# Storing the soft max's split parts from GpSimd's DMA queue, with a new set of stream priorities

## The chip, the cores and the metric

The kernel runs on one core of one Trainium2 chip. The metric is the device time of one execution in microseconds (us), lower is better. The engines are called as in the profile: PE is TensorE's matmul and PEld its weight load, DVE is VectorE, ACT is ScalarE, POOL is GpSimd, SP is SyncE. SPq and POOLq are the instruction queues of SP and POOL where they issue DMAs.

## What is computed

Three layers follow one another. An attention with landmarks (Nystrom) over 4 batches and 8 heads of 576 tokens of 64, a mixture of 8 experts of which each token goes to the best one, and a dense layer with a leaky activation:

```
q_lm, k_lm = means of 18 tokens, 32 landmarks          # per batch and head
A  = softmax(q    @ k_lm.T / 8)                        # 576 x 32
Bm = softmax(q_lm @ k_lm.T / 8)                        # 32 x 32
C  = softmax(q_lm @ k.T    / 8)                        # 32 x 576
Z  = Bm.T / (norm1 * norminf);  6 times: Z = 2 Z - Z @ Bm @ Z
x  = A @ Z @ C @ v                                     # 2304 tokens of 512
e  = argmax(x @ w_gate);  keep the first `capacity` tokens of each expert
y  = gate * (relu(x @ w1[e]) @ w2[e])                  # 512 -> 1024 -> 512
h  = y @ w_in;  g = max(h, 0) + alpha * min(h, 0)      # 512 -> 2048
out = g @ w_out                                        # 2048 -> 512
```

w_in and w_out arrive as 64-bit floats, and the kernel narrows them itself.

## The kernel before

Work is written as streams: Python generators that yield one operation at a time (an instruction with its engine and an estimate of its duration). `Plan.run` lays the streams out ahead of time into one fixed order for each engine. Of the operations that could start at about the same planned time on an engine it takes that of the stream with the lowest rank (ranks closer than 30 ns of planned start compete; otherwise the earlier start wins). Each engine and each DMA queue then runs its order strictly front to back, and an instruction that waits holds everything behind it. So a changed rank, a changed engine or a changed duration moves instructions on all engines. Line L74, at which nearly all rows stand, is the helper that issues every operation.

The stages of the first pass are:

- **Attention.** For each batch b four head pairs are turned (`turn`: loads of q and k come in from SP, PE transposes them, ACT moves them to `qkT`, PE averages the landmarks, DVE copies those to `half`, which PE transposes too). For each of the 8 groups (b, g) of four heads, `attend_c` makes C, Bm and C @ v (rows named mx, nm, EC, EB, CT, Ys), and `attend_a` makes A. The latter's steps are, in order: scores into PSUM (`big`); DVE transposes them to `T1` (rows say T); DVE takes the maxima `amx`; an engine subtracts them (T<-T,amx); ACT takes the exponential; DVE sums (`asum`) and scales (T<-T,asum); DVE transposes to `AT`; ACT rounds AT to 16 bits (`parts[:, 0]`); an engine subtracts to get the rest (`parts[:, 1]`); a DMA stores both parts to `xdram` in DRAM. Batch 0 keeps its parts in `xT` itself, so its rows say xT for parts. xdram is read back only when a later expert is fetched (`prefetch`, xT<-xdram).
- **post0** (`attention_post([0])`) runs Z's six steps for batch 0 (rows RW), makes the router's logits (mm<-Gm,AT), finds the expert of the first token (`e0`), and routes. From `e0` on SP may load that expert's W1 (stream `weights`), and `landmark_rows` multiplies W1 with the landmarks' values (big<-W,MT); for that it needs both `big` buffers of PSUM, which the attention's groups use too. `post` does the same for the three other batches.
- **moe_h, moe_y, moe2_h, moe2_out** (stream `first`, then `out`) are the expert and the dense layer for batch 0. `moe_h` multiplies xT with W1's rows (MW); `moe_y` multiplies with W2 and turns its five tiles to `yT`; `moe2_h` takes 16 slices f of w_in against yT, in two column ranges: A (256 columns, tiles 0 and 1) and B (320 columns, the other tiles). `columns(..., ahead)` gives the order: the first `ahead` slices in range A, the same slices in range B, then both ranges slice by slice. `moe2_out` multiplies with w_out (WO).
- **w_in and w_out** are prepared beside all that: 64-bit words come in by SP (the first ten rows to a stage in hgA by stream `early`, the others to `st`), DVE narrows them (int32 rows), ACT takes sums of squares, and `split` makes two 16-bit halves of each pair. A split of kind "d" is one ACT instruction and one DVE instruction; kind "a" is two ACT instructions and one on POOL. `convert(..., low)` gives pair k the kind `low[k % len(low)]`.
- **The loop** then repeats expert and dense layer for each further pair of batch and expert that has tokens (twice with these inputs), with an order of its own. While the first pass's `moe2_out` runs, `first_next`, `next_w1` and `next_w2` fetch and split the weights of the loop's first round.

In `run`, the streams' ranks are given as numbers; the attention's are RANKS[b][g] - 1.768 for `attend_c`, RANKS[b][g] + 4.328 for `attend_a`, and RANKS[b][hp // 2] + 0.943 for `turn`.

Of the kernel before, what the change touches and what calls it, by code (L numbers as in the profile page):

```python
# [10 lines left out]
I32 = mybir.dt.int32  # L11
AF = mybir.ActivationFunctionType
ALU = mybir.AluOpType
# [4 lines left out]
P = 128  # L18
TP = 64
TJ = 9  # L20
BLOCKS = (8, 1, 3, 5, 7, 0, 2, 4, 6)
LM = 32
AT0 = 512 - 10 * LM - LM
RANKS = [[2.735, 1.638], [2.359, 2.122], [2.325, 2.315], [3.168, 3.56]]
MAXF = 3.0e38
GAP = 2
EARLY = 12
# [338 lines left out]
class Kernel:  # L366
# [124 lines left out]
    def loads(self):  # L491

        for b in range(self.B):
            for hp in range(self.H // 2):
                for nm, src in (("k", self.k), ("q", self.q), ("v", self.v)):
                    self.raw[nm, b, hp] = t = yield Get(self.S["v" if nm == "v" else "qk"])
                    yield self.dq.dma_start(t, src[b, 2 * hp : 2 * hp + 2].rearrange("h (p j) d -> (h p) j d", j=TJ))
                    self.have.add((nm, b, hp))
                    if (nm, b, hp) == ('v', 0, 0):
                        self.tc.prologue_barrier()  # L500
# [156 lines left out]
    def attend_a(self, b, g):  # L657

        act, dve = self.act, self.dve

        def t(name, n):
            return self.ap.tile([P, n], F32, tag=name, name=f"{name}{b}{g}", bufs=2)

        yield self.until(("T", b, 2 * g), ("T", b, 2 * g + 1))
        T1 = yield Get(self.S["T1"])
        SA = yield Get(self.big)
        SAf = SA.rearrange("p a n -> p (a n)")
        yield self.scores(SAf, b, g, 1, 0, False)
        yield from self.scored(b, g)
        yield dve.transpose(T1, SAf[:, AT0 + LM : 768])  # L670
        yield Put(SA)
        T13 = T1.rearrange("p (c m) -> p c m", m=32)
        amx, asum = t("amx", 18), t("asum", 18)
        yield dve.tensor_reduce(amx, T13, axis=AX.X, op=ALU.max)
        yield (self.gp, dve)[1].tensor_tensor(T13, T13, amx.unsqueeze(2).to_broadcast([P, 18, 32]), op=ALU.subtract)
        yield act.activation(T1, T1, AF.Exp, scale=0.125)
        yield dve.tensor_reduce(asum, T13, axis=AX.X, op=ALU.add)
        yield dve.tensor_scalar(asum, asum, 1e-9, 1.0 / ASCALE, op0=ALU.add, op1=ALU.mult)
        yield dve.reciprocal(asum, asum)
        yield (self.gp, dve)[1].tensor_tensor(T13, T13, asum.unsqueeze(2).to_broadcast([P, 18, 32]), op=ALU.mult)  # L680
        self.AT[b, g] = AT = yield Get(self.S["AT"])
        yield dve.transpose(AT, T1)
        yield Put(T1)
        self.have.add(("A", b, g))

        parts = self.xT[:, g] if b == 0 else (yield Get(self.S["parts"]))
        yield act.copy(parts[:, 0], AT)
        yield (self.gp, dve)[0].tensor_tensor(parts[:, 1], AT, parts[:, 0], op=ALU.subtract)
        self.have.add(("P", b, g))
        yield self.dq.dma_start(self.xdram[b][:, g], parts).after(1.0)  # L690
        if b:
            yield Put(parts)
        self.have.add(("stored", b, g))

    def attention_post(self, bs):

        pe, act, dve, E = self.pe, self.act, self.dve, self.E
        a2 = self.a2
        b = bs[0]
# [58 lines left out]
        for it in range(6):  # L758
            ps = yield Get(self.mm)
            rp = ps[:, : 64 * G].rearrange("p (g m) -> p g m", g=G)  # L760
            n = 1 if it == 5 else 2
# [15 lines left out]
        for _ in range(2):  # L777
            x = yield Get(self.mm)
# [22 lines left out]
        for _ in range(2):  # L801
            x = yield Get(self.mm)
# [26 lines left out]
        for n, bb in enumerate(bs):  # L829
            yield self.until(("A", bb, 0), ("A", bb, 1))  # L830
            AT = [self.AT[bb, g] for g in range(2)]
# [11 lines left out]
        self.have.add(("x", bs[-1]))  # L843
        if b:
            yield self.until(("routed", 0))
            self.streams["post"].own = 3.503
        yield from self.route(bs, L)

    @staticmethod
# [335 lines left out]
    def early(self):  # L1185


        src, n = self.source_in, self.n_early
        stage = self.hg[0].rearrange("p k a n -> p (k a n)").bitcast(I32)
        stage = [stage[:, 2048 * k : 2048 * k + 2048].rearrange("p (k n two) -> p k n two", k=2, two=2) for k in range(2)]  # L1190
        loaded, used = set(), set()

        def loads():
            for i in range(0, n, 2):
                yield Until(lambda: i < 4 or i - 4 in used)
                for k in range(2):
                    yield self.dq.dma_start(stage[i // 2 % 2][:, k].rearrange("p n two -> p (n two)"), src(i + k).bitcast(I32)).after(6.0)
                loaded.add(i)

        yield Fork(loads())  # L1200
        kids = []
        for i in range(0, n, 2):
            yield Until(lambda: i in loaded)
            yield from self.narrow(stage[i // 2 % 2], self.pair("wi", i))
            used.add(i)
            kids.append((yield Fork(self.squares("wi", i))))
        yield ended(kids)
        self.have.add("early")
# [213 lines left out]
    def moe2_h(self, first=False):  # L1422
        act, dve, hg = self.act, self.dve, self.hg
# [18 lines left out]
            yield Put(ps)  # L1442

        self.h = {}
        for x in self.columns("wi", 16, self.tiles, 5 if first else 4):
            if isinstance(x, Until):
                yield x
                continue
            if x[1]:
                self.have.add("wide")  # L1450
            ps = yield Get(self.mm)
            yield self.product(ps, *x)
            self.h[x[:2]] = yield Fork(activated(ps, *x))
# [91 lines left out]

    def weight_in(self):
        yield self.until("rooms", "early")
        yield from self.weight2("wi", self.source_in, self.amax, 'dad', self.n_early)

    def source_in(self, i):  # L1550

# [58 lines left out]
    def run(self):  # L1610
# [14 lines left out]
        with tc.manual_schedule(engines={ET.PE, ET.DVE, ET.Activation, ET.Pool, ET.SP}):  # L1625
# [19 lines left out]
                parts=Slots(self.a2, "parts", [P, 2, 576], F16, bufs=2),  # L1645
                AT=Slots(self.a2, "AT", [P, 576], bufs=6),
# [4 lines left out]
            for _ in range(10):  # L1651
# [1 line left out]
            self.streams = {  # L1653
                "loads": Stream(self.loads(), 0),
                "turn": Stream(self.turn(), 2),
                "constants": Stream(self.constants(), 8.156),
                "post0": Stream(self.attention_post([0]), 2.155),
                "first": Stream(self.pre(), 3.29),
                "weights": Stream(self.weights(), 8.016),
                "rooms": Stream(self.rooms(), 9.297),  # L1660
                "post": Stream(self.attention_post(list(range(1, self.B))), 3.108),
                "early": Stream(self.early(), 11.284),
                "wi": Stream(self.weight_in(), 8.393),
                "wo": Stream(self.weight_out(), 10.574),
                "clear": Stream(self.clear(), 2.147),
                "experts": Stream(self.experts(), 2.517),
                "out": Stream(self.first_out(), 4.43),
                "next": Stream(self.first_next(), 3.207),
                "next_w1": Stream(self.next_w1_late(), 2.351),
                "next_w2": Stream(self.next_w2('d'), 3.573),  # L1670
            }
            for b in range(self.B):
                for g in range(2):
# [8 lines left out]
        n = nc.values_load(self.lst[0:1, 0:1], min_val=0, max_val=self.PAIRS - 1)  # L1682
# [34 lines left out]
```

## Time and profile before

| | us |
|---|---|
| median of 3 runs | 559.45 |
| lowest, highest run | 558.52, 567.44 |
| profiled execution, its own time | 559.79 |
| span of the profiled execution | 558.1 |
| PE busy in the span | 524.8 |
| DVE busy | 307.5 |
| ACT busy | 266.9 |
| POOL busy | 54.7 |

The span is what the trace covers; the 1.7 us between it and the execution's own time lie around the program. Busy times are sums of instruction durations; PE's instructions are pipelined, so that a busy PE need not be at its peak. In rows of instructions "x6" is a count, "<-" stands between what is written and what is read, and a bracket tells how long the engine sat idle before the instruction and what ended that. PEclk is the granted clock of TensorE as a share of full speed.

### The profile page before, as it was taken

The numbers are of one execution on the slowest core, as the hardware profiler recorded it, in microseconds if no ns is written. First come the engines' busy times: TensorE is split into PE (matmuls) and PEld (weight loads), VectorE is DVE, ScalarE is ACT, GpSimd is POOL, SyncE is SP. The second block draws the span as 40 slices with busy tenths as digits, with TensorE's granted clock in tenths as the row PEclk, the third lists the DMA queues.
The fourth block names the chain that finished last, engine by engine and source line by source line (L and its number), as shares of the span: only waits on it lengthen the run. The fifth ranks groups of instructions, "written<-read, shape, count | busy, mean of one in ns | idle before, by whom it ended". The sixth has DMA issues, their size and how long they took to land.

```text
span 558.1 us, 13933 instructions
## 1 busy us (share of the span) xinstructions
PE 524.8 (94%) x5750; PEld 350.4 (63%) x5750; DVE 307.5 (55%) x744; ACT 266.9 (48%) x581; POOL 54.7 (10%) x78
## 2 busy tenths in 40 slices
PE   8798898898999998999999999999999999999995
PEld 6576676476449786544675667754466566775444
DVE  1877778878899998906052459630004355962000
ACT  4564545685476656756043397520013349751000
POOL 4100000100013432101000000001010000000101
PEclk9988879999999999999999999999999999999999
DMA  8858666714649630656000320000005050000000
GB/s 281 247 172 292 205 211 188 236 55 152 228 153 315 191 137 2 172 196 175 38 11 1 119 76 1 1 0 20 38 31 156 1 176 19 1 1 1 38 20 30
DMA packets 36396, 61.21 MB, mean 110 GB/s; under 512 B 6032, under 2 KB 15632, under 8 KB 36336
## 3 DMA queue, kind: packets, MB, share of 16 engines
q1 hardware_dynamic: 35232, 56.80, 32.2%
q0 software_dynamic: 1104, 3.54, 1.7%
q8 instruction: 46, 0.75, 0.6%
q14 instruction: 14, 0.11, 0.1%
HBM read 49.50 MB, written 10.62 MB: 108 GB/s over the span
## 4 chain that ended last, share of the span: by engine, by line
PE 66%; DVE 15%; issue 7%; DMA 6%; ACT 3%; SPq 2%; POOL 0%; POOLq 0%; ACTq 0%; DVEq 0%
PE mm L74 63%; PE big L74 2%; DMA st<-in_moe_w_in 2%; DVE W L74 2%; DMA out<-st,idxc 2%; DMA qk<-in_k 2%; SPq L74 2%; DVE MW L74 1%; DVE WIa L74 1%; DVE WIb L74 1%; DVE mm L74 1%; PE mm L1619 1%; DVE hgA L74 1%; ACT junk L74 1%; DVE g L74 1%
## 5 line engine op out<-in xcount | busy, mean ns | idle before, releaser
L74 PEld LDWEIGHTS <-hgA 128*128 128x128 f16 (+1 forms) x864 | 71.0, 102 | 66.6 <-issue 3.8
L74 PE MATMUL mm<-yT,WIa 128*128 128x256 f16 (+1 forms) x864 | 109.2, 286 | 3.5 <-DVE MW L74 1.3
L74 PEld LDWEIGHTS <-WIa 128*128 128x128 f16 x864 | 83.5, 98 | 27.3 <-issue 4.7
L74 PE MATMUL mm<-WO,hgA 128*128 128x512 f16 (+1 forms) x432 | 73.0, 344 | 0.4 <-issue 0.4
L74 PE MATMUL mm<-W,hgA 128*128 128x512 f16 (+1 forms) x432 | 73.3, 344 | 0.0
L74 PE MATMUL mm<-WO,hgB 128*128 128x512 f16 (+1 forms) x432 | 72.6, 344 | 0.0
L74 ACT ACTIVATE st<-mm,fac 128x512 f32<-128x512 f32 (+1 forms) x15 | 9.7, 644 | 106.2 <-PE mm L74 106.2
L74 PEld LDWEIGHTS <-hgB 128*128 128x128 f16 (+1 forms) x432 | 36.1, 102 | 33.7
L74 ACT ACTIVATE g<-mm 128x256 f32<-128x256 f32 (+1 forms) x96 | 39.3, 414 | 12.5 <-PE mm L74 11.4
L74 DVE SCALAR_TENSOR_TENSOR mm<-g,oma,mm 128x256 f32<-128x256 f32 (+1 forms) x80 | 40.3, 514 | 3.8 <-ACT g L74 2.5
L74 PE MATMUL mm<-xT,MW 128*128 128x320 f16 (+1 forms) x288 | 37.1, 286 | 4.8 <-DVE hgA L74 2.5
L74 POOL DMA_INDIRECT out<-st,idxc x12 | 12.2, 1015 | 297.1 <-ACT st L74 277.5
L74 PE MATMUL mm<-yT,WIb 128*128 128x256 f16 (+1 forms) x288 | 36.2, 286 | 0.4 <-DVE hgB L74 0.4
L74 PEld LDWEIGHTS <-MW 128*128 128x128 f16 x288 | 27.7, 98 | 12.7 <-issue 3.3
L74 DVE COPY idxc<-idxn 128x5 int32<-128x5 int32 x2 | 0.3, 172 | 64.0 <-issue 46.3
L74 PE MATMUL mm<-id,qk 128*128 128x128 f32 x160 | 28.0, 311 | 7.3 <-DVE half L74 3.4
L74 ACT COPY qkT<-mm 128x512 f32<-128x512 f32 (+1 forms) x48 | 25.4, 551 | 18.3 <-PE mm L74 18.0
L74 ACT ACTIVATE junk<-mm 128x512 bf16<-128x512 f32 (+1 forms) x27 | 15.5, 572 | 39.1 <-PE mm L74 38.8
L74 PEld LDWEIGHTS <-WIb 128*128 128x128 f16 x288 | 28.1, 98 | 7.5 <-issue 0.4
L74 PEld LDWEIGHTS mm<-id,qk 128*128 128x128 f32 x160 | 20.4, 157 | 11.5 <-DVE half L74 6.6
L74 ACT ACTIVATE hgA<-mm 128x256 f16<-128x256 f32 (+1 forms) x48 | 19.5, 411 | 17.0 <-PE mm L74 16.9
L74 DVE SCALAR_TENSOR_TENSOR hgA<-mm,hgA 128x256 f16<-128x256 f32 (+1 forms) x48 | 21.4, 455 | 10.1 <-ACT hgA L74 10.0
(284 smaller groups left out, 715.0 us busy)
## 6 DMA issues: line engine op xcount, KB each, us to landing
W<-in_moe_w SPq DMA_DIRECT2D x8, 1024.0 KB, 6.9
st<-in_moe_w_out SPq DMA_DIRECT2D x16, 512.0 KB, 4.1
hgA<-in_moe_w_in SPq DMA_DIRECT2D x10, 512.0 KB, 6.5
qk<-in_k SPq DMA_DIRECT2D x16, 288.0 KB, 4.5
qk<-in_q SPq DMA_DIRECT2D x16, 288.0 KB, 4.9
v<-in_v SPq DMA_DIRECT2D x16, 288.0 KB, 4.4
out<-zero SPq DMA_DIRECT2D x18, 256.0 KB, 4.5
W<-in_moe_w SPq DMA_DIRECT2D x8, 512.0 KB, 4.5
```

The costliest lines, as they stand in the source:

```text
L74: r = getattr(self.lane.engine, name)(*a, **k)
L1619: nc.tensor.matmul(o[:, :256], self.ones16, self.zero.bitcast(F16), start=True, stop=True)
```

## The change

Of the instructions, six places change. Expressions of the form `(self.dq, self.gp)[i]` pick SP's queue for 0 and POOL's for 1; `nm == ""` is never true.

1. `attend_a`: the store of the parts goes from SP's queue to POOL's (8 DMAs).
2. `attend_a`: the subtraction of the maxima goes from DVE to POOL (8 instructions), and that which makes the lower part goes from POOL to DVE (8 instructions).
3. `moe2_h` of the first pass: `ahead` is 3 in place of 5.
4. `weight_in`: w_in's eight pairs are split "d" throughout, in place of "d", "a", "d" in turn (the pairs 1, 4 and 7 change).
5. `next_w2`: W2's four pairs are split "d", "a" in turn, in place of "d" throughout (the pairs 1 and 3 change).
6. Ranks: the attention's groups (0, 0), (1, 0) and (1, 1), and eleven of the streams.

The lines in `loads` and `early` change in form only.

```diff
-RANKS = [[2.735, 1.638], [2.359, 2.122], [2.325, 2.315], [3.168, 3.56]]
+RANKS = [[2.837, 1.638], [3.158, 2.149], [2.325, 2.315], [3.168, 3.56]]
...
-                    yield self.dq.dma_start(t, src[b, 2 * hp : 2 * hp + 2].rearrange("h (p j) d -> (h p) j d", j=TJ))
+                    yield (self.dq, self.gp)[nm == ""].dma_start(t, src[b, 2 * hp : 2 * hp + 2].rearrange("h (p j) d -> (h p) j d", j=TJ))
...
-        yield (self.gp, dve)[1].tensor_tensor(T13, T13, amx.unsqueeze(2).to_broadcast([P, 18, 32]), op=ALU.subtract)
+        yield (self.gp, dve)[0].tensor_tensor(T13, T13, amx.unsqueeze(2).to_broadcast([P, 18, 32]), op=ALU.subtract)
...
-        yield (self.gp, dve)[0].tensor_tensor(parts[:, 1], AT, parts[:, 0], op=ALU.subtract)
+        yield (self.gp, dve)[1].tensor_tensor(parts[:, 1], AT, parts[:, 0], op=ALU.subtract)
         self.have.add(("P", b, g))
-        yield self.dq.dma_start(self.xdram[b][:, g], parts).after(1.0)
+        yield (self.dq, self.gp)[1].dma_start(self.xdram[b][:, g], parts).after(1.0)
...
-            self.streams["post"].own = 3.503
+            self.streams["post"].own = 3.568
...
-        for x in self.columns("wi", 16, self.tiles, 5 if first else 4):
+        for x in self.columns("wi", 16, self.tiles, 3 if first else 4):
...
-        yield from self.weight2("wi", self.source_in, self.amax, 'dad', self.n_early)
+        yield from self.weight2("wi", self.source_in, self.amax, 'd', self.n_early)
...
-                "constants": Stream(self.constants(), 8.156),
-                "post0": Stream(self.attention_post([0]), 2.155),
+                "constants": Stream(self.constants(), 8.105),
+                "post0": Stream(self.attention_post([0]), 3.27),
...
-                "post": Stream(self.attention_post(list(range(1, self.B))), 3.108),
-                "early": Stream(self.early(), 11.284),
+                "post": Stream(self.attention_post(list(range(1, self.B))), 3.015),
+                "early": Stream(self.early(), 11.316),
...
-                "wo": Stream(self.weight_out(), 10.574),
-                "clear": Stream(self.clear(), 2.147),
-                "experts": Stream(self.experts(), 2.517),
-                "out": Stream(self.first_out(), 4.43),
-                "next": Stream(self.first_next(), 3.207),
+                "wo": Stream(self.weight_out(), 10.863),
+                "clear": Stream(self.clear(), 2.619),
+                "experts": Stream(self.experts(), 2.117),
+                "out": Stream(self.first_out(), 7.555),
+                "next": Stream(self.first_next(), 2.2),
...
-                "next_w2": Stream(self.next_w2('d'), 3.573),
+                "next_w2": Stream(self.next_w2('da'), 2.369),
```

## Rows read from the trace of the kernel before

**Rows 1.** Busy time of each engine by stage, in the order of the columns: the stretch (us from the span's start), its length, busy time and count of PE, PEld, DVE, ACT and POOL, the granted clock, the DMA engines' share, GB/s.

```profile
20.00:90.00 70.00, 60.37 (x1285) 46.55 (x1286) 52.48 (x145) 35.38 (x84) 7.10 (x6) 0.85 0.69 222
...
141.00:168.00 27.00, 25.75 (x215) 13.52 (x214) 24.46 (x46) 16.26 (x31) 2.17 (x1) 1.00 0.56 199
168.00:228.60 60.60, 58.12 (x557) 46.72 (x553) 56.17 (x135) 40.28 (x89) 20.15 (x18) 1.00 0.51 157
228.60:278.60 50.00, 49.31 (x326) 24.73 (x323) 17.85 (x28) 23.20 (x37) 5.02 (x5) 1.00 0.49 150
278.60:558.10 279.50, 270.65 (x1986) 172.83 (x1986) 107.13 (x274) 107.35 (x250) 10.65 (x11) 1.00 0.11 37
```

**Rows 2.** The chain of work that ended last, its longest pieces from moe2_h's end on: start, length, what.

```profile
217.75 60.18 PE mm L74 x413
...
278.62 25.64 PE mm L74 x201
...
369.18 45.71 PE mm L74 x282
```

**Rows 3.** What SP's queue waited for over the whole run: in total, times, longest; then SP's timeline around batch 2's first store.

```profile
SPq L74 <- PE mm L74: 69.8, 19, 9.8
SPq L74 <- POOL parts L74: 28.6, 6, 10.2
```

```profile
79.96 0.38 SPq L74 DMA_DIRECT2D qk<-in_q  x1
84.17 0.34 SPq L74 DMA_DIRECT2D xdram<-parts  x1
85.62 1.31 SPq L74 DMA_DIRECT2D W<-in_moe_w  x2
```

**Rows 4.** POOL's groups of instructions, kept apart by shape: count, busy us in total, mean ns of one, idle time before them.

```profile
L74 POOL DMA_INDIRECT out<-st,idxc x12 | 12.2, 1015 | 297.1 <-ACT st L74 277.5 <-DMA W<-in_moe_w 11.0 <-DMA out<-st,idxc 8.6
L74 POOL TENSOR_TENSOR parts<-AT,parts 128x576 f16<-128x576 f32 x6 | 7.7, 1279 | 72.7 <-ACT parts L74 72.7
L74 POOL TENSOR_TENSOR WIa<-WIa 128x1024 f16<-128x1024 f32 x2 | 4.9, 2454 | 45.2 <-ACT WIa L74 45.2
L74 POOL TENSOR_TENSOR WIb<-WIb 128x1024 f16<-128x1024 f32 x1 | 2.2, 2224 | 0.8 <-PE mm L74 0.8
```

**Rows 5.** The instructions that touch T, amx and xdram, by tile: count, shortest/median/longest in ns, first and last start.

```profile
L74 DVE TENSOR_TENSOR T<-T,amx x8: 735/758/760, 16.7 to 109.0; 128x576 f32<-128x576 f32 x8
L74 SPq DMA_DIRECT2D xdram<-parts x6: 343/344/350, 52.9 to 118.6; - x6
L74 SPq DMA_DIRECT2D xT<-xdram x1: 345/345/345, 237.5 to 237.5; - x1
```

**Rows 6.** DVE's timeline in the attention: the transposes that free T1 in the groups (2, 0) and (2, 1) (AT<-T), and those that fill it again in the last two groups (T<-big).

```profile
78.90 0.76 DVE L74 STREAM_TRANSPOSE AT<-T 128x576 f32<-128x576 f32 x1
95.62 0.78 DVE L74 STREAM_TRANSPOSE AT<-T 128x576 f32<-128x576 f32 x1
98.64 0.77 DVE L74 STREAM_TRANSPOSE T<-big 128x576 f32<-128x576 f32 x1
107.29 0.77 DVE L74 STREAM_TRANSPOSE T<-big 128x576 f32<-128x576 f32 x1
```

**Rows 7.** Where a DVE instruction that is short elsewhere takes long beside one of POOL: nm and fac by tile (ns, shortest/median/longest), the same for W<-st,W, and the timelines of POOL and DVE.

```profile
L74 DVE TENSOR_SCALAR nm<-mx x8: 169/441/893, 13.5 to 106.9; 128x2 f32<-128x2 f32 x8
L74 DVE SCALAR_TENSOR_TENSOR fac<-gate,pyr,wfac x5: 200/207/1481, 152.5 to 178.7; 128x1 f32<-128x1 f32 x5
L74 DVE SCALAR_TENSOR_TENSOR W<-st,W x10: 1207/1224/2490, 150.7 to 192.1; 128x1024 int32<-128x1024 int32 x10
```

```profile
163.09 2.17 POOL L74 TENSOR_TENSOR WIa<-WIa 128x1024 f16<-128x1024 f32 x1 [44.55 <-ACT WIa L74]
174.09 2.73 POOL L74 TENSOR_TENSOR WIa<-WIa 128x1024 f16<-128x1024 f32 x1 [0.69 <-ACT WIa L74]
163.86 2.49 DVE L74 SCALAR_TENSOR_TENSOR W<-st,W 128x1024 int32<-128x1024 int32 x1
175.36 1.48 DVE L74 SCALAR_TENSOR_TENSOR fac<-gate,pyr,wfac 128x1 f32<-128x1 f32 x1
```

**Rows 8.** The two kinds of split, DVE's and ACT's share, by shape: count, busy us, mean ns.

```profile
L74 DVE SCALAR_TENSOR_TENSOR WIa<-WIa,s_wi 128x1024 f16<-128x1024 f32 x3 | 3.8, 1274 | 0.0
L74 ACT CAST WIa<-WIa 128x1024 f16<-128x1024 f32 x2 | 2.1, 1040 | 0.8 <-DVE WIa L74 0.8
```

**Rows 9.** The start of moe2_h on PE and DVE: range A's second and third products, the logits, the last tile of yT, and the block of products behind them.

```profile
176.39 1.49 PE L74 MATMUL mm<-yT,WIa 128*128 128x256 f16 x12
178.03 2.26 PE L74 MATMUL mm<-Gm,AT 128*64 128x8 f32 x36
180.23 12.25 PE L74 MATMUL mm<-yT,WIa 128*128 128x256 f16 x96
178.28 0.47 DVE L74 COPY yT<-mm 128x256 f16<-128x256 f16 x2
```

**Rows 10.** What PE and its weight loads waited for in the attention (0 to 108 us), in total, times, longest; then the granted clock of two stretches of 10 us (columns as in rows 1).

```profile
PE mm L74 <- DVE half L74: 3.4, 5, 1.6
PEld mm L74 <- DVE half L74: 6.6, 9, 1.7
```

```profile
70.00:80.00 10.00, 8.84 (x198) 7.34 (x193) 9.23 (x31) 3.85 (x8) 0.00 (x0) 0.79 0.74 225
80.00:90.00 10.00, 10.00 (x154) 7.65 (x154) 5.28 (x24) 4.45 (x11) 1.28 (x1) 0.70 0.54 171
```

**Rows 11.** post0's end and what hangs on it: e0 on DVE, W1's last two loads on SP, the product that needs them on PE.

```profile
76.55 0.14 DVE L74 TENSOR_SCALAR e0i<-m 1x1 int32<-1x1 f32 x1
99.07 1.40 SPq L74 DMA_DIRECT2D W<-in_moe_w  x2
108.31 1.95 PE L74 MATMUL big<-W,MT 64*32 64x512 f32 x32
```

```profile
W<-in_moe_w SPq DMA_DIRECT2D x16, 256.0 KB, 5.3
```

More of the change, by code (lines that the diff above doesn't have):

```diff
@@ L1196, in loads @@
                 for k in range(2):
-                    yield self.dq.dma_start(stage[i // 2 % 2][:, k].rearrange("p n two -> p (n two)"), src(i + k).bitcast(I32)).after(6.0)
+                    yield (self.dq, self.gp)[0].dma_start(stage[i // 2 % 2][:, k].rearrange("p n two -> p (n two)"), src(i + k).bitcast(I32)).after(6.0)
                 loaded.add(i)
```

## The prediction

> **What bounds the kernel now.** I read the stages first, then the chain that ended last, then the queues that the change touches. In the stages [rows 1] the reader is to compare PE and DVE. From 278.6 us on, PE is busy 270.7 of 279.5 us, and from 228.6 to 278.6 it is busy 49.3 of 50. The chain [rows 2] says the same: from 217.75 us it is nearly all PE in unbroken blocks, the first of 60.18 us. Nothing in the loop is edited, and its order is laid out separately. So all behind 228.6 us (558.1 - 228.6 = 329.5 us) is taken as fixed, and the question is when w_out's products, which begin at 228.6, can begin.
>
> The 228.6 us before them have two parts. From 141 to 228.6 us DVE is busy 24.46 + 56.17 = 80.6 of 87.6 us (92%) and PE 83.9 (96%): here extra work on DVE counts nearly in full. In the attention neither is full: from 20 to 90 us PE is busy 60.4 and DVE 52.5 of 70 us, PE's granted clock averages 0.85 of its full 2.4 GHz, and DMA engines are busy 69% [rows 1]. There the two engines wait for each other. PE and its weight loads stood 3.4 + 6.6 = 10.0 us behind DVE's copies to half [rows 10]. That is where an order matters more than a duration.
>
> **Store on POOL's queue.** SP's queue stood 28.6 us before six stores whose parts POOL had not finished [rows 3]. What stood behind it is to be read from SP's timeline: what follows the store at 84.17 us is weight loads (85.62), not loads of q, k or v. SP waits much more, 69.8 us, for PE to free load buffers [rows 3]. So I put the freed time at 0, with W1's earlier loads as a reserve that comes back below. The issue itself costs SP 0.34 us each [rows 5]. On POOL the nearest row is the indirect store, 1.015 us [rows 4], so 8 x 1.0 = 8 us of an engine that is busy 7.1 of 70 us between 20 and 90 [rows 1]. Covered by POOL's idle time: 0 on the path; without that cover, 8 us. When the data land matters to nobody until xT is read back at 237.5 us [rows 5].
>
> **The two subtractions change places.** Off DVE go 8 x 0.758 us [rows 5]; onto it come 8 subtractions of the same 128 x 576 elements. Their type (f32 minus f16) is not in the trace on DVE; I take 0.758 again, so DVE +-0 (bounds: half and double the row, -3 to +6 us). POOL gives 8 x 1.28 and takes 8 x 1.28 [rows 4]: 0. The chain of one group grows by 1.28 - 0.76 = 0.5 us, and by one store of 1.0 us if that stands in front of it in POOL's queue. What waits for this chain is the next user of its T1 buffer (there are two). The buffer of group (2, 0) was free at 79.66 and written again at 98.64; the last group's was free at 96.40 and written at 107.29 [rows 6]. With 10.9 to 19.0 us of slack, 1.5 us are hidden: 0.
>
> POOL's subtractions also hold DVE up: nm, two elements per partition, takes 0.169 us alone and up to 0.893 [rows 7]. Eight such subtractions stay eight, at other moments: 0, with +-8 x 0.72 = +-5.8 us as bounds.
>
> The Trainium skill, page "SBUF — State Buffer", section "SBUF: two separate sides", speaks against this store: a DMA issued from GpSimd has its descriptors written by GpSimd, which VectorE locks out while it runs a two-port instruction. No row of before has such a store beside a busy DVE. By that rule each issue would be late by the rest of the DVE instruction that it meets. The time would still be POOL's, which is idle.
>
> **Splits of w_in.** Pairs 1, 4 and 7 cost DVE 3 x 1.274 = +3.8 us and spare ACT 3 x 1.04 us [rows 8] and POOL 4.9 + 2.2 = 7.1 us [rows 4]. But two of the three POOL instructions had stopped DVE: the narrowing at 163.86 took 2.49 us against a median of 1.22, and fac at 175.36 took 1.48 against 0.21, both beside POOL's WIa [rows 7]. That gives back 2 x 1.27 = 2.5 us. Net +1.3 us on a DVE that is 93% busy from 168 to 228.6 [rows 1]: +1.2 us. Bounds: 0, if ACT's relief lets DVE run closer; +3.8, if the stalls only move.
>
> **Splits of W2 for the loop.** DVE -2 x 1.27, ACT +2 x 1.04, POOL +2 x 2.2 to 2.5 us, in the stretch from 228.6 to 278.6 us, where they are busy 17.9, 23.2 and 5.0 of 50 us [rows 1]: 0. If the cover were gone, the loop's first round would start up to 2 x 2.2 us late.
>
> **ahead = 3.** moe2_h then comes to range B after its third product, and B needs the last yT tile, done at 178.28 + 0.47 = 178.75. The third product ended at 177.88, and the logits' product from 178.03 to 180.29 covered the rest [rows 9]: 0. Without that cover PE would wait 0.9 us.
>
> **Ranks.** post0 goes from 2.155 to 3.27. The turns' ranks are RANKS + 0.943: 3.09 for the half (1, 1), 3.27 and 3.26 for batch 2. Before, post0 went ahead of every turn; now it goes behind these three. The rows of before have the price of the old order: around 76 to 87 us, when post0's tail and the routing run, PE's clock falls to 0.79 and 0.70 in two stretches of 10 us, (0.21 + 0.30) x 10 = 5.1 us of full clock lost, and the waits for half make 10.0 us over the attention [rows 10]. I cannot lay out the new order by hand. Bounds: all of the 5.1 us plus a quarter of the 10.0 us, -7.6; or the same in the other direction, +7.6, if a late post0 crowds what follows. I take a third of the gain, -2.5 us. The other ranks (out, next, experts, clear) move work into stretches where PE is full and others are not: 0.
>
> **Sum.** +1.2 - 2.5 = -1.3 us on a span of 558.1: 556.8, and with the 1.7 us around it 558.5 for such an execution. The profiled execution (559.79) stands 0.34 over the median (559.45), so 558 us.
>
> **The rivals.**
>
> 1. *The attention tightens.* With turns ahead of post0, PE stays fed and its clock up. At stake from 20 to 108 us are 10.0 us of waits [rows 10] and 0.15 x 70 = 10.5 us of clock [rows 1]. If 60% of the 20.5 us come back: -12 us, with the +1.2 us about 547 to 548. For it: DVE is 75% busy there, so the waits are order, not load. Against it: SP's 69.8 us for free buffers and DMA engines at 69%, which are not touched.
>
> 2. *post0 comes too late (slower).* e0 was found at 76.55 us; W1's last loads were issued at 99.07 to 100.47 and landed after 5.3 us, about 105.4; the product with W1 began at 108.31 [rows 11]. Slack: 2.9 us, plus the 4.2 us that SP sat from 80.34 to 84.17 and its 0.34 us issue there [rows 3], so about 7 us. Once e0 is found after 83.6 us, each us later delays W1's product and moe_h. A group of the attention takes some 13 us (eight by 108 us); one group late: 13 - 7 = +6, with +1.2 about 566 us; two groups late: +19, 579 us. For it: post0's six steps are a chain that any higher rank can interrupt. Against it: ranks decide only between operations ready within 30 ns.
>
> 3. *DVE pays in full.* The POOL stalls return elsewhere: +3.8 for w_in, no gain in the attention, and a few us for T's subtraction where DVE has nothing else ready: 563 us. For it: DVE is 92% busy behind 141 us.
>
> 4. *POOL's queue starves (the rule of the page cited above).* Stores late in POOL's queue hold the next group's subtraction: 0.5 + 1.0 + the 0.7 that nm lost beside POOL [rows 7] = 2.2 us a group, 17.8 us over eight if nothing hid them, 576 us. It decides only from 10.9 us of lateness on [rows 6], so I give it little.
>
> That the change does nothing it says can't be: eight stores leave SP's queue. That they free nothing is part of my forecast.
>
> **How the numbers follow.** Forecast (555 to 562 us) 0.55; rival 1, 0.17; rival 2, 0.13, half of it with two groups late; rival 3, 0.12; rival 4, 0.03. About 2% (11 us) is what a measurement of this kernel tells from no change. Faster by over 2% (below 548.3) is two thirds of rival 1: 0.11. Slower by over 2% (above 570.6) is half of rival 2, rival 4 and a little of rival 3: 0.10. The rest, 0.79, is within 2%. The range leaves out one in ten on each side: 548 to 570 us.
>
> **What would show it.** Right: w_out's first product at 226 to 229 us and the loop unchanged behind it; DVE's busy total near 306 us (307.5 + 1.3 - 2.5) and POOL's near 60 (54.7 + 8 - 7.1 + 4.5); SP no longer waiting for POOL; no stall of fac; the clock between 70 and 90 us above 0.8. Wrong: W1's product well after 108 us with e0 after 84 (rival 2); T<-T,amx on POOL far over 1.3 us, or DVE idle before asum (rivals 3 and 4); a loop that is longer or starts with a wait for W2.

## The result, and the profile after

The change makes the kernel 0.5 to 1% slower, not faster: a median of 562.98 us (559.92 to 565.94, 12 runs) against 559.05 us for the kernel before beside it, ratio 1.0109, 95% interval 1.0074 to 1.0145. A second set of runs, beside more runs of before, gave 1.0051 (1.0018 to 1.0083). Executions over 1.5% above the fastest of their kernel and set are left out of all ratios and means here (23 of before's 113, one of after's 24); with all in but one of 1066 us, after's mean is 2.9 us above before's, at mean clocks of 0.9811 and 0.9833.

The stages of after, columns as in [rows 1]:

```profile
20.00:90.00 70.00, 61.56 (x1483) 49.05 (x1483) 56.67 (x154) 37.92 (x89) 16.20 (x31) 0.95 0.76 246
90.00:108.00 18.00, 13.00 (x252) 9.24 (x252) 12.07 (x33) 7.61 (x20) 2.31 (x2) 0.77 0.63 181
141.00:168.00 27.00, 26.30 (x234) 14.45 (x236) 25.81 (x47) 17.77 (x30) 0.00 (x0) 1.00 0.47 165
168.93:232.48 63.55, 57.88 (x517) 45.82 (x516) 57.41 (x134) 37.94 (x86) 15.86 (x16) 0.97 0.46 142
282.41:561.30 278.89, 270.65 (x1986) 172.58 (x1985) 107.14 (x274) 107.17 (x250) 10.73 (x11) 1.00 0.11 36
```

The loop takes 278.89 us, before 279.50 [rows 1]: as forecast, all behind w_out's products is unchanged. The loss is ahead of them. moe2_h begins at 168.93 (before 168.53) but ends at 232.48 (before 228.60). Up to 90 us after looks better, PE's granted clock is 0.95 in place of 0.85; from 90 to 108 it looks worse, 0.77 with PE busy 13.0 of 18 us (before 1.00 and 14.3).

What stands around the moved operations: T and the stores on POOL (by tile, as [rows 5]), DVE's waits before asum and before pairsi (constants that POOL makes) from 15 to 120 us (in total, times, longest; then the one of before), and SP's timeline when e0 is known (then the later loads of before):

```profile
L74 POOL TENSOR_TENSOR T<-T,amx x8: 1150/1380/2062, 17.2 to 105.3; 128x576 f32<-128x576 f32 x8
L74 POOL DMA_DIRECT2D xdram<-parts x6: 539/557/622, 53.6 to 113.7; - x6
```

```profile
DVE asum L74 <- ACT T L74: 4.5, 4, 2.4
DVE pairsi L74 <- POOL pairsi L74: 1.7, 1, 1.7
```

```profile
DVE asum L74 <- ACT T L74: 0.6, 1, 0.6
```

```profile
81.24 1.31 SPq L74 DMA_DIRECT2D W<-in_moe_w  x2
82.59 0.58 SPq L74 DMA_DIRECT2D hgA<-in_moe_w_in  x1
83.36 4.06 SPq L74 DMA_DIRECT2D W<-in_moe_w  x6
```

```profile
93.68 1.25 SPq L74 DMA_DIRECT2D W<-in_moe_w  x2
99.07 2.04 SPq L74 DMA_DIRECT2D W<-in_moe_w  x3
107.93 0.39 SPq L74 DMA_DIRECT2D W<-in_moe_w  x1
```

The six stores of the batches 1 to 3 take POOL 0.54 to 0.62 us each, the two of batch 0 0.58 and 0.80. The subtraction took 0.758 us on DVE [rows 5] and takes 1.15 to 2.06 us on POOL, and DVE, which waited 0.6 us for the exponential behind it in before, now waits 4.5 us. SP issues all eight loads of W1 and W2 (4 MB) within 6.2 us; in before they lay between 85.62 and 108 us, W2's two behind 99.07 [rows 3, 11].

In moe2_h PE waits five times, 5.5 us in all (before four times, 2.5 us, shown below it):

```profile
188.57 8.98 PE L74 MATMUL mm<-yT,WIa 128*128 128x320 f16 x72 [0.70 <-DVE hgA L74]
200.15 0.49 PE L1619 MATMUL mm<-zero,ones 128*128 128x256 f16 x3 [1.91 <-DVE g L74]
208.10 6.04 PE L74 MATMUL mm<-yT,WIa 128*128 128x320 f16 x48 [1.45 <-DVE hgA L74]
215.16 4.73 PE L74 MATMUL mm<-yT,WIa 128*128 128x320 f16 x36 [0.89 <-DVE hgB L74]
227.91 4.73 PE L74 MATMUL mm<-yT,WIb 128*128 128x320 f16 x36 [0.55 <-DVE hgB L74]
```

```profile
194.04 8.98 PE L74 MATMUL mm<-yT,WIa 128*128 128x320 f16 x72 [0.86 <-DVE hgA L74]
210.67 3.10 PE L74 MATMUL mm<-yT,WIa 128*128 128x320 f16 x24 [0.85 <-DVE hgB L74]
214.10 1.79 PE L74 MATMUL mm<-yT,WIa 128*128 128x320 f16 x12 [0.33 <-DVE hgB L74]
217.75 1.79 PE L74 MATMUL mm<-yT,WIb 128*128 128x320 f16 x12 [0.43 <-DVE hgB L74]
```

### The profile page after: what moved, and what is told of

The parts are those of the page before. It is cut to its first block, busy times and chain, and to the rows that moved or that the text cites. A ratio compares the mean times of both kernels' runs of the same rounds, so it can differ in the third digit from the quotient of the medians.

```text
span 561.3 us, 13978 instructions
## 1 busy us (share of the span) xinstructions
PE 527.5 (94%) x5774; PEld 351.9 (63%) x5774; DVE 307.2 (55%) x745; ACT 265.6 (47%) x580; POOL 58.4 (10%) x85
## 4 chain that ended last, share of the span: by engine, by line
PE 62%; DVE 17%; issue 9%; DMA 5%; ACT 4%; SPq 2%; POOL 1%; POOLq 0%; ACTq 0%; DVEq 0%
PE mm L74 59%; DVE WIa L74 2%; DVE W L74 2%; DMA out<-st,idxc 2%; SPq L74 2%; PE big L74 2%; DVE MW L74 2%; DMA qk<-in_q 1%; PE mm L1619 1%; ACT junk L74 1%; DVE WIb L74 1%; DVE hgA L74 1%; DMA st<-in_moe_w_out 1%; DVE mx L74 1%; DMA qk<-in_k 1%
## 5 line engine op out<-in xcount | busy, mean ns | idle before, releaser
L74 PE MATMUL mm<-yT,WIa 128*128 128x320 f16 (+1 forms) x864 | 110.7, 289 | 4.5 <-DVE hgA L74 2.2
L74 PE MATMUL mm<-id,qk 128*128 128x128 f32 x160 | 25.9, 288 | 9.5 <-DVE half L74 4.6
L74 PEld LDWEIGHTS mm<-id,qk 128*128 128x128 f32 x160 | 18.3, 145 | 16.3 <-DVE half L74 8.9
L74 ACT ACTIVATE hgA<-mm 128x256 f16<-128x256 f32 (+1 forms) x48 | 19.0, 415 | 13.5 <-PE mm L74 13.5
```

The lines of the kernel that those rows point to most:

```text
L74: r = getattr(self.lane.engine, name)(*a, **k)
```

## The experiments

**How the times are split.** Every execution comes with its span and its mean granted clock. Within one kernel the span falls by some 3.7 us for each 0.01 of mean clock (one line through all executions, each kernel about its own mean). So a kernel's excess over before (mean of 90 executions: 558.07 us, clock 0.9860) is split into *clock* (365 us times the difference of mean clocks), *around* (time less span) and *order* (the rest, at the same clock). The split is an estimate; the order's standard error is 0.3 to 0.6 us, 0.95 for the engines without a new order.

| kernel | ratio to before, 95% | mean clock | us over before | clock | order | around |
|---|---|---|---|---|---|---|
| after (both sets) | 1.0109 and 1.0051, above | 0.9816 | +4.2 | +1.6 | +2.0 | +0.6 |
| store alone | 1.0064 (1.0030 to 1.0099) | 0.9809 | +3.0 | +1.9 | +1.1 | 0.0 |
| engines, no new order | 1.0167 (1.0127 to 1.0206) | 0.9782 | +8.7 | +2.9 | +6.0 | -0.2 |
| ranks alone | 1.0094 (1.0053 to 1.0136) | 0.9797 | +3.9 | +2.3 | +1.2 | +0.4 |
| after, old ranks | 1.0103 (1.0067 to 1.0139) | 0.9877 | +4.8 | -0.6 | +5.5 | -0.1 |
| after, w_in split as before | 1.0041 (1.0007 to 1.0076) | 0.9830 | +3.1 | +1.1 | +2.2 | -0.2 |
| after, ahead 5 | 1.0029 (0.9991 to 1.0067) | 0.9854 | +2.9 | +0.2 | +2.2 | +0.4 |
| after, both of these | 1.0105 (1.0050 to 1.0159) | 0.9802 | +6.1 | +2.1 | +3.7 | +0.3 |
| after, stores on SP | 1.0050 (1.0017 to 1.0083) | 0.9833 | +3.7 | +1.0 | +2.8 | -0.1 |
| after, W2 held | 1.0048 (1.0015 to 1.0081) | 0.9843 | +3.0 | +0.6 | +2.2 | +0.2 |
| after, narrowing earlier | 1.0056 (1.0020 to 1.0093) | 0.9861 | +3.1 | 0.0 | +2.8 | +0.3 |

**Engines and ranks apart.** In the first two kernels the plan is made as in before and only the queue differs from which an instruction is issued (`.on` names it): for the store alone, then for the store and both subtractions. The third has the old engines and the new ranks, the fourth all of after but the ranks.

```diff
-        yield self.dq.dma_start(self.xdram[b][:, g], parts).after(1.0)
+        yield self.dq.dma_start(self.xdram[b][:, g], parts).after(1.0).on(self.gp)
...
-        yield (self.gp, dve)[1].tensor_tensor(T13, T13, amx.unsqueeze(2).to_broadcast([P, 18, 32]), op=ALU.subtract)
+        yield (self.gp, dve)[1].tensor_tensor(T13, T13, amx.unsqueeze(2).to_broadcast([P, 18, 32]), op=ALU.subtract).on(self.gp)
...
-        yield (self.gp, dve)[0].tensor_tensor(parts[:, 1], AT, parts[:, 0], op=ALU.subtract)
+        yield (self.gp, dve)[0].tensor_tensor(parts[:, 1], AT, parts[:, 0], op=ALU.subtract).on(dve)
```

> The kernel before with its order on PE, DVE and ACT as it is; only the eight stores of parts are issued on GpSimd. Theory B (the burst): without the stores, SP issues W1's and W2's eight loads close together, the DMA engines are full in a stretch of 10 us before 108, PE stands or runs at half clock behind it, W1's product is later than 108.3, and the span is 1 to 3 us longer than before (559 to 561). Theory O (order and splits): the store by itself is hidden; W1's product at 108.3 +-0.7, w_out's first product at 228.6 +-1, ratio 1.000 +-0.003. Theory Q (POOL's queue): T's users wait for POOL's stores; DVE idles more in the attention, +2 us or more.

> As the store alone, and the two subtractions change engines too; order, ranks, splits and ahead are those of before. Theory O (order and splits): as before, ratio 1.000 to 1.004; w_out's first product at 228 to 230. Theory S (the swapped subtraction): POOL's subtraction of amx is in the chain of a group and takes up to 2 us where DVE took 0.76, so the attention without an order of its own for it ends 2 to 4 us later than with the store alone (ratio 1.004 to 1.008).

> The kernel before with only the ranks of after: stores on SP, subtractions and splits as before. Theory R (the ranks cost): e0 is found near 80, the last narrowings of w_in's first part come late (115 us instead of 92), moe_h begins later; the time is that of after, ratio 1.006 to 1.012. Theory O, in the form that the splits of w_in cost: moe2_h stays at 60 us and the time is that of before, ratio 0.997 to 1.003.

> The kernel after with the ranks of before: stores and subtractions moved, w_in's splits all on DVE, ahead 3. Theory R (the ranks cost): moe_h and the attention go back to their times of before, ratio 0.998 to 1.003. Splits: moe2_h still takes 63 us where before takes 60.1, w_out's first product is near 231 to 232, ratio 1.006 to 1.012.

None of the three parts is free. The store alone costs +3.0 us, of which 1.9 us go with a lower clock; W1's product comes at 106.09 us there, not later than 108.31 as theory B had it, and moe_h begins at 118.80 at clock 0.93. The swapped subtractions, in the same order, then add 5.7 us, 4.9 of them order. DVE's waits of this run from 15 to 120 us and its e0, and below them those of the store alone (spans of 573.4 us at clock 0.961 and 565.7 at 0.966, both above their kernel's mean):

```profile
DVE asum L74 <- ACT T L74: 6.6, 5, 1.8
DVE pairsi L74 <- POOL pairsi L74: 6.2, 1, 6.2
79.90 0.14 DVE L74 TENSOR_SCALAR e0i<-m 1x1 int32<-1x1 f32 x1
```

```profile
DVE asum L74 <- ACT T L74: 1.6, 2, 1.1
73.68 0.14 DVE L74 TENSOR_SCALAR e0i<-m 1x1 int32<-1x1 f32 x1
```

That is 5.0 us more before asum, and one wait of 6.2 us for constants: POOL, which made pairsi at 7.63 us in before, makes it at 23.74 here, behind its first subtraction at 17.83. e0 comes 6.2 us later, as much as that one wait alone. So the cost that theory S forecast is there and larger, but its cause is not shown: these runs don't tell the waits before asum from the one for the constants, which is 1.7 us in after. The ranks alone gain nothing on the old engines (+3.9 us; e0 comes at 88.31 us, the last narrowing of w_in's first part at 100, moe2_h takes 60.09 us at clock 1.00 as in before, where after's plan with the old ranks takes 63.55 at 0.97 as after does). On the new engines they do: order 5.5 with the old ranks, 2.0 with the new, but 2.2 us of that go back as clock (0.9877 to 0.9816), so that in time the two hardly differ.

**The same kernels again.** after and before once more, unchanged.

> The kernel after, unchanged, for a second profile and for the clock of the kernel before on the same chip. Theory C (clock): of the 4 us, about half goes with the mean granted clock (0.981 against 0.985) and falls in other places than in the first profile. Theory M (moe2_h): the same five waits of PE between 168 and 229 us as in the first profile (0.70, 1.91, 1.45, 0.89, 0.55 us) stand again, whatever the clock did.

> The kernel before, unchanged, for a second profile. Theory C (clock): the stretches at half clock lie elsewhere in the attention, the span moves by about 5 us for each 0.01 of mean clock. Theory M: moe2_h takes 60.1 us at full clock with waits of PE of 0.86, 0.85, 0.33 and 0.43 us, the same as in the first profile; how long the attention takes differs by less than 3 us.

Theory C holds in that clock is part of the difference in the split (0.9816 against 0.9860; over all executions only 0.9811 against 0.9833, so how much of it is the kernel's is not shown), with 3.7 us for each 0.01 instead of some 5; the stretches at half clock moved, one into moe2_h of before (61.67 us in place of 60.07). Of the five waits four stand again (0.87, 1.91, 0.90, 0.55), the one of 1.45 us does not. The second profiles give what single ones can't: how the start of moe_h depends on the clock up to there. The stretch from 0 to moe_h's first product in before, in after, and in four kernels of after's engines and ranks (ahead 5; W2 held; narrowing earlier; the same with ahead 5 and the old splits, edits that come into play behind moe_h's start), columns as in [rows 1]:

```profile
0.00:118.89 118.89, 101.70 (x2231) 77.75 (x2232) 84.13 (x226) 65.14 (x149) 16.35 (x44) 0.93 0.69 219
```

```profile
0.00:120.17 120.17, 103.57 (x2309) 79.74 (x2310) 84.06 (x226) 61.17 (x141) 23.24 (x52) 0.93 0.74 236
```

```profile
0.00:121.18 121.18, 104.39 (x2309) 80.41 (x2310) 84.24 (x226) 61.00 (x141) 23.30 (x52) 0.93 0.73 234
```

```profile
0.00:114.88 114.88, 98.88 (x2310) 77.10 (x2311) 83.82 (x226) 60.75 (x141) 23.24 (x52) 0.97 0.72 212
```

```profile
0.00:117.28 117.28, 100.28 (x2344) 77.37 (x2345) 84.33 (x227) 62.71 (x144) 23.61 (x51) 0.97 0.74 237
```

```profile
0.00:114.91 114.91, 100.05 (x2344) 77.42 (x2344) 84.55 (x227) 62.65 (x144) 23.65 (x51) 0.97 0.77 243
```

(The first of these is before's second profile.) At one clock, 0.93, moe_h begins at 118.9 in before and at 120.2 to 121.2 in after's order: 1.3 to 2.3 us later, though its last T<-big stands at 103.53 where before has 107.29 [rows 6]. (before's first profile has 119.11 at 0.91.) So the 3.8 us by which the attention seems to end earlier bring no earlier moe_h. The lateness itself isn't resolved: the two kernels of the last two rows have one order up to moe_h and one clock, 0.97, and lie 2.4 us apart.

**moe2_h.** Each of the two edits undone, then both.

```diff
-        for x in self.columns("wi", 16, self.tiles, 3 if first else 4):
+        for x in self.columns("wi", 16, self.tiles, 5 if first else 4):
-        yield from self.weight2("wi", self.source_in, self.amax, 'd', self.n_early)
+        yield from self.weight2("wi", self.source_in, self.amax, 'dad', self.n_early)
```

> The kernel after with w_in split as before (every third pair on ACT and POOL). Theory M (the splits): PE's waits in moe2_h fall back to about 2.5 us, moe2_h takes 60 to 61 us instead of 63.5, w_out's first product comes 2.5 to 3.5 us earlier than in after, ratio to before 1.002 to 1.006. Theory A (ahead): the waits stay, moe2_h 63 to 64 us, ratio 1.008 to 1.014.

> The kernel after with moe2_h's ahead 5 as before instead of 3. Theory A (ahead): moe2_h 60 to 61 us, ratio to before 1.002 to 1.006. Theory M (the splits): moe2_h 63 to 64 us with the wait of 1.9 us still there, ratio 1.008 to 1.014.

> The kernel after with both edits of moe2_h undone (w_in's third pairs on ACT and POOL, ahead 5); the order up to moe_y is that of after. Theory M (those two edits cost): at full clock moe2_h and the products of w_out behind it take 110.1 us as in before, where after takes 111.8; ratio to before 1.002 to 1.005. If the loss is only in the attention and the clock: ratio 1.005 to 1.010, the same as after.

With one edit undone moe2_h takes 60.59 (splits) or 59.55 us (ahead; w_out's products then take 51.2 instead of 50), all at clock 1.00; with both undone 65.07 us at clock 0.95, with a wait of 2.83 us for the router's rows. So it isn't the splits or ahead in themselves: theories M and A both fall as single causes. Each plan interleaves the router, the splits and moe2_h another way, and PE's waits range from 2.5 (before) to 5.8 us over them.

**The burst of weight loads.** PE's timeline of after around 98 us, and two stretches of 10 us in after, then in before:

```profile
97.34 0.75 PE L74 MATMUL big<-qkT 64*32 64x352 f32 x4
100.44 2.40 PE L74 MATMUL big<-qkT 64*32 64x352 f32 x26 [2.35 <-issue]
```

```profile
90.00:100.00 10.00, 6.78 (x176) 5.36 (x169) 6.48 (x21) 5.47 (x13) 1.15 (x1) 0.99 1.06 297
100.00:110.00 10.00, 8.22 (x108) 4.71 (x111) 6.51 (x14) 3.42 (x9) 1.71 (x2) 0.50 0.16 58
```

```profile
90.00:100.00 10.00, 8.14 (x204) 6.35 (x201) 9.07 (x18) 6.54 (x16) 1.28 (x1) 1.00 0.71 219
100.00:110.00 10.00, 8.03 (x218) 5.02 (x216) 8.54 (x19) 5.54 (x14) 1.27 (x1) 1.00 0.72 207
```

PE stops in the middle of a group of products, waiting for nothing that the profile shows, while the DMA engines are full; behind that its clock is 0.50 (before 1.00). Four kernels take the burst apart: stores back on SP; W2's loads held behind a store of 512 bytes that waits for later data, in after, in the store alone, and in after with the earlier narrowing (next paragraph). The data is the first square of W1's product (diff below) or, in the last two, the seventh transpose AT.

```diff
-        yield self.until("early")
+        yield self.until("early", "landmarks")
+        yield self.dq.dma_start(self.scr, self.ss["w1"][:, 0:1])
         yield from self.load_expert(bass.ds(e0, 1), ["w2"])
```

> The kernel after in its planned order, but the eight stores of parts are issued on SP where the plan has them. Theory B (the burst): with the stores back in SP's queue the eight loads of W1 and W2 are spread again, DMA engines are below 0.9 in 90 to 100 us, PE does not stand over 2 us on issue near 98, the clock from 100 to 110 us is above 0.8 instead of 0.50, and the time is 1.5 to 3 us under that of after. Theory E (the last narrowing of w_in's first part holds moe_h): moe_h still begins at 119.5 to 120.5 and the time is that of after within 1 us.

> The kernel after, its order on every engine unchanged; in SP's queue a store of 512 bytes that waits for the first square of W1's product (near 110 us) stands in front of W2's two loads, so that these are no part of the burst. Theory B (the burst): no stand of PE over 2 us near 98, clock from 100 to 110 us above 0.8, 1.5 to 3 us faster than after unless W2 then comes too late for its first scaling near 120 to 130. Theory E: nothing before 120 changes by more than 1 us.

> The run with the store alone, every engine's order as there (that is: as in before); in SP's queue a store of 512 bytes that waits for the seventh transpose AT (near 100 us) stands in front of W2's two loads. Theory B (the burst): PE's stand on issue of 2.6 us near 103 and the half clock behind it go, the mean granted clock of the runs is back at 0.985 or more, ratio 0.998 to 1.003. If the burst is not what costs: mean clock 0.980 to 0.982 and ratio 1.004 to 1.010 as with the store alone.

> The kernel after with the narrowing of w_in's first part ahead of the last two turns, order as in that run, and W2's two loads held behind the seventh transpose AT. Theories B and E together: no stand of PE near 100, moe_h begins near 116, ratio 0.999 to 1.003, under both after and the run with the narrowing alone. If the burst costs nothing: 1.003 to 1.009 as with the narrowing alone.

With W2 held to 104.84 us the DMA engines' share from 90 to 100 us is 0.38, and no stand on issue over 1 us is left near 98; but the ratio, 1.0048, is that of after's second set. With the stores back on SP the stand is there all the same (2.90 us, with the DMA engines busy 0.15 of it), and the clock from 100 to 110 us is 0.66. The store alone with W2 held gave 1.0078 (1.0033 to 1.0122), no better than without; there ACT stood 5.66 us for W2, whose sums of squares are in its queue ahead of MW. The fourth gave 1.0130 (1.0071 to 1.0188), and its stand had moved to where the loads now are:

```profile
120.86 1.07 PE L76 MATMUL mm<-RW 32*32 32x64 f32 x31 [6.08 <-issue]
```

So PE's stand moved with the loads in that kernel, but theory B's price isn't shown: taking the burst away brought nothing that these runs resolve. before has such stands too, at other places, 4.5 us in all of those of 0.5 us or more, where after has 3.4:

```profile
47.84 0.24 PE L74 MATMUL mm<-RW 32*32 32x64 f32 x1 [2.53 <-issue]
61.11 0.65 PE L74 MATMUL mm<-v,CT 64*32 64x64 f32 x31 [1.98 <-issue]
```

What ends them can be read from the DMA queue that the profile calls instruction, which moves packets of 16 KB. In the stand of 6.08 us it moved nothing from 114.8 to 118.5 us; its one packet of 118.5 to 119 us (packets, MB, share of the 16 engines there) is

```profile
q8 instruction: 1, 0.02, 12.3%
```

and PE goes on at 120.86. Over 19 profiles of these kernels PE has 50 stands on issue of 0.5 us or more, and in 49 it goes on 2.2 to 2.9 us after the start of such a packet (in one 3.4). That PE waits there for its own instructions fits all of these rows, also the stand of 2.90 us beside nearly idle DMA engines; what makes a packet late, and what such a stand costs in the end, no run here shows.

**The last narrowing.** In after the last rows of w_in's first part are narrowed at 115 to 118.6 us (before 92), and moe_h waits for them. First their stream was put ahead by rank, in after and in after with the old ranks; then only the time which the plan adds behind their loads was cut.

```diff
-                "early": Stream(self.early(), 11.316),
+                "early": Stream(self.early(), 8.01),
...
-                    yield (self.dq, self.gp)[0].dma_start(stage[i // 2 % 2][:, k].rearrange("p n two -> p (n two)"), src(i + k).bitcast(I32)).after(6.0)
+                    yield (self.dq, self.gp)[0].dma_start(stage[i // 2 % 2][:, k].rearrange("p n two -> p (n two)"), src(i + k).bitcast(I32)).after(1.0)
```

> The kernel after with one rank changed: the stream that loads and narrows w_in's first part goes ahead of W1's loads (8.01 instead of 11.316), so that its last narrowing comes near 95 instead of 118 us. Theory E (this narrowing holds moe_h): moe_h begins 2 to 3 us earlier, near 117, moe2_h begins near 166 instead of 168.9, 2 to 3 us faster than after. Theory D (DVE's whole work sets the start of moe2_h): moe_h begins earlier, moe2_h does not (168 to 170), the time is that of after.

> The kernel after with the ranks of before, and w_in's first part ahead of W1's loads. Theory E: the attention of the run with the old ranks (last transposes near 94.5) is no longer followed by late narrowings at 117 to 119, moe_h begins 3 to 6 us earlier than 120, the time is 2 to 5 us under that run, at or below before. Theory D: moe2_h begins at 167 to 168 as in that run, same time.

> The kernel after with one figure of the plan changed: the time that it adds behind the loads of w_in's first part is 1 us instead of 6, which puts the last narrowing ahead of the attention's last two turns in DVE's order, as in before; ranks, e0 and all up to there stay. Theory E (this narrowing holds moe_h): moe_h begins 2 to 3 us earlier than in after, near 117.5, moe2_h near 166.5, ratio to before 1.000 to 1.004. Theory D (DVE's whole work sets moe2_h's start): moe_h begins earlier, moe2_h at 168 to 170 as before, ratio 1.005 to 1.010.

> The kernel after with the earlier narrowing and ahead 5. Theories E and M together: moe2_h begins near 166.5, moe2_h and w_out's products take 110.7 us as in the run with ahead 5, ratio 0.998 to 1.002. Theory D: no better than ahead 5 alone, 1.003 +-0.003.

> The kernel after with the earlier narrowing, w_in's splits and ahead of before: what is left of the change are the engines and the ranks. Theories E and M together: 0.996 to 1.001, the attention's gain arrives. Theory D: 1.002 to 1.006.

The first two, both with rank 8.01, took 584.98 and 589.46 us (ratios 1.0433 and 1.0558): the stream then also passes the constants (8.105 and, with the old ranks, 8.156), which post0 needs, and e0 is found at 112.56 and 108.66 us. They say nothing of theory E. The third moves the narrowing alone, to 107.4; moe_h begins at 117.28 and moe2_h at 165.31, as theory E said. But its clock up to there is 0.97, and after's order at 0.97, without the earlier narrowing but with W2 held, begins moe_h at 114.88 (rows above): the 3 us can be the clock's. Its time shows no gain either, 1.0056 with an order of +2.8. So theory E isn't borne out. DVE has no wait before asum from 15 to 120 us in this kernel, and the order's part is no smaller than after's. With ahead 5 as well the ratio is 1.0116 (1.0064 to 1.0168), with ahead 5 and the old splits 1.0167 (1.0118 to 1.0216): the parts don't add up, and no version of after beats before.

## Why the prediction was wrong, step by step

- **What is fixed** was right: loop and w_out's products are unchanged, and the loss lies ahead of them. Several signs came, too (DVE 307.2 us busy, POOL 58.4, e0 at 80.0, no stall of fac), but w_out's first product, at 232.48 instead of 226 to 229, did not.
- **The terms at 0 for the moved operations** are the step that failed. Without the ranks' -2.5 us the sum stands 1.2 us over before; after with the old ranks, the kernel of that sum, took 4.8 us over before (1.0103).
- **"The two subtractions change places ... with 10.9 to 19.0 us of slack, 1.5 us are hidden: 0"** asked when T1's buffer is filled next [rows 6]. But each group's own asum stands in DVE's queue a few instructions on, and DVE takes its queue in order: it waits there for POOL and ACT, 4.5 us in after against 0.6. Put on top of the store in before's order, the swap cost 5.7 us; the one wait for POOL's constants, which the prediction left out too, can be all of it. That the waits before asum are what after's +2.0 us of order consist of isn't shown, and the earlier narrowing speaks against it: there they are gone, and the order is +2.8. The prediction had named the sign ("DVE idle before asum") for rivals 3 and 4, and 563 us, rival 3's time, is what came, but by luck: rival 3 goes by more work on DVE, whose total is 307.2 us (before 307.5).
- **Store at 0**: right for POOL (0.54 to 0.80 us each, less than the 1.0 us estimated), wrong as a whole: +3.0 us alone. "The freed time at 0" overlooked that W1's and W2's loads then go out together; but with W2 held the store alone still gave 1.0078, so by what it costs stays open.
- **Port stalls, a term of 2.5 us**: those of the splits did go. fac took 199 to 215 ns (before up to 1481 [rows 7]). Those of the attention only moved. nm takes 168 to 170 ns, where in before it lost 2.4 us over eight, but other DVE instructions now take long beside POOL's subtraction (the narrowing WIa<-hgA,WIa takes 1.22 us elsewhere, NB's subtraction of 128x192 took 0.36 in before):

```profile
51.96 1.72 POOL L74 TENSOR_TENSOR T<-T,amx 128x576 f32<-128x576 f32 x1 [9.16 <-DVE amx L74]
52.58 2.18 DVE L74 SCALAR_TENSOR_TENSOR WIa<-hgA,WIa 128x1024 int32<-128x1024 int32 x1
105.47 1.16 DVE L74 TENSOR_TENSOR NB<-eye,rsum 128x192 f32<-128x192 f32 x1
```

  With NB of 128x64 (0.87 us, 0.22 in before) and a 1x1 subtraction (0.86, 0.14) that is 3.1 us lost on DVE. POOL's subtractions themselves take 11.7 us for eight, where DVE took 6.1 [rows 5].
- **Splits, +1.2 us**: moe2_h takes 63.55 us against 60.07; about 1.9 of the difference is its clock, 0.97. What is left is 1.6 us in this profile and 0.3 in the second (62.22 us at 0.97): near the size forecast. Two kernels with the same splits and ahead show moe2_h at clock 1.00: 61.16 us (narrowing earlier) and 60.84 (that and W2 held), 1.1 and 0.8 over before. By the runs above it belongs rather to the plan's interleaving than to the splits in themselves.
- **Ranks, -2.5 us**: mis-sized, and of the other sign on the old engines: -0.6 us on after's engines (+4.8 to +4.2), +3.9 alone. The clock from 70 to 90 us rose to 0.80 and 0.86 (before 0.79 and 0.70 [rows 10]), as the text asked for, but fell to 0.50 from 100 to 110; waits for half grew from 10.0 to 13.5 us in the same 108 us. The ranks fit the new engines (order 5.5 to 2.0) and pay back part of what these cost there.
- **Rival 2** was tried by accident: with e0 36 us later (112.56), slack 7 us, its rule gives moe2_h 29 us later; it began 29.3 us later (197.84 against 168.53). The second such kernel doesn't bear it out: with e0 at 108.66 the rule gives 25 us, and moe2_h began 30.0 us later (198.53).

What stays open: by which wait the store and the swap cost their time, why the mean clock of most variants is lower than before's (0.978 to 0.985 against 0.986), and why about 0.6 us more lies around the span in after. The split of after's loss into order, clock and around rests on a fitted line, and single terms of 1 us are not settled by it.

## What to carry to other kernels

Slack of a buffer isn't slack of a step: before an operation goes to another engine, look for its next consumer in every in-order queue, above all in the queue it leaves, and for what now stands behind it in the queue it joins. A planned order is tuned to its engines; compare stages of two single profiles only after their granted clock up to there is compared, and then expect a scatter (here 2.4 us). And a queue that is set free issues the next transfers at once: ask what they collide with.

## What was not expected of the hardware

- A store from POOL's queue lands later: 5.1 us from issue to landing (median of 6 x 288 KB) where the same stores from SP took 2.5; with the store alone 5.3, back on SP 2.4.
- The Trainium skill's rule that the prediction cited (page "SBUF — State Buffer", section "SBUF: two separate sides") doesn't show in the issue, 539 to 622 ns for these six; whether it is behind the later landing no run here tells.
- PE stood for up to 6.08 us in mid-group with nothing to wait for that the profile shows; 49 of 50 such stands ended 2.2 to 2.9 us after the start of a 16 KB packet in the instruction queue.
- POOL's subtraction of 128x576 took 1.15 us or up to 2.06, with the same shapes, and beside it a DVE subtraction of one element took 0.86 us (0.14 in before).
